# Another pairing of attention heads, and the transfers that follow from it, in a fused attention and feed-forward kernel

## The chip, the cores and the metric

The kernel runs on one core of a Trainium2 chip. The metric is the device time of one execution in microseconds (us). Three timed runs before the change took 405.54, 406.10 and 406.79 us; the median is 406.1 us. A profiled execution of the same program is shown beside them.

The core has engines that each run a queue of their own and wait for each other by semaphores: TensorE (PE in the profile, with its weight loads as PEld), VectorE (DVE), ScalarE (ACT), GpSimd (POOL) and SyncE (SP). SP computes nothing here; it issues transfers, in the order of its queue. The transfers run on 16 DMA engines.

## The reference

Attention with normalised queries and keys, then a feed-forward layer with a gated activation:

```python
# q, k, v: (8, 12, 448, 64) float32; w_in: (768, 2048); w_out: (2048, 768)
q_n = q / (np.linalg.norm(q, axis=-1, keepdims=True) + 1e-06)
k_n = k / (np.linalg.norm(k, axis=-1, keepdims=True) + 1e-06)
scores = np.matmul(q_n, k_n.transpose(0, 1, 3, 2)) / tau          # tau = 0.1
scores = scores - np.max(scores, axis=-1, keepdims=True)
attn = np.exp(scores)
attn = attn / (np.sum(attn, axis=-1, keepdims=True) + 1e-09)
attn_out = np.matmul(attn, v)
x = attn_out.transpose(0, 2, 1, 3).reshape(B * S, H * D)          # (3584, 768)
h = x @ w_in
g = h * np.clip(h + 3.0, 0.0, 6.0) / 6.0
out = g @ w_out                                                   # (3584, 768) float32
```

## The kernel before

**Pairs and twins.** The 12 heads of a batch are worked on in 6 pairs, so there are 48 pairs in all, numbered i = 0 to 47. A pair is worked on as one: its two heads fill the 128 rows of a tile, 64 each, in the transposed queries and keys and in the transposed attention output `xT`, whose chunk `hp` of 128 rows is the left operand's contraction in the first feed-forward product. Which two heads make a pair therefore decides which rows of `w_in` belong to which partition. In the kernel before, pair n of a batch holds heads n and n + 6. Two pairs, 2d and 2d + 1, make a twin d.

**Items.** The inputs of a twin's attention are loaded as two items j = 2d and 2d + 1, one of q and one of k; there are 48 items of 448 KB (four heads of 448 x 64 float32). An item's tile has 128 partitions: 64 for each of the two pairs of the twin, and on each partition, for both heads g = 0, 1 of the pair, seven rows of 64 numbers (1,792 bytes in one piece of memory). `load_qk` (line 189) issues an item's load on SP. The seven buffers `raws` (five from item 26 on) hold items; a load waits until the item that used its buffer last has been normalised (line 190).

An item is then squared (`square`, line 211, on ACT, POOL or DVE), reduced to sums of squares on DVE (`reduce`, line 228), its inverse norms are made on ACT (`norms`, line 246), and it is multiplied by them (`normalise`, line 266, mostly on POOL). It is transposed by TensorE at first and, from item 14 on, by a crossbar transfer that SP issues (`crossbar`, line 325). `scores`, `exps` and `values` (lines 395, 428, 453) make the attention of a pair, and `back_crossbar` or `back_two` (lines 504, 515) bring its output into `xT`, again by crossbar transfers on SP.

**Values.** `load_v` (line 201) loads a twin's four heads by four transfers on SP: for each g the two heads of that place in their pairs, and for each of them the two halves of the sequence, on 64 partitions each, shifted against each other so that both end in tiles of 4 x 64 numbers. Zeros are put beside them at the start (lines 966 to 968). `vcast` (line 285) turns a pair's two heads into bf16 on POOL or DVE; before, they lie at places i % 2 and i % 2 + 2 of the twin's tile.

**Weights.** `next_weights` (line 908) issues the next entry of a list on POOL's queue, which also casts float32 to bf16: four pieces of `w_in`, then four of `w_out`, each of 768 KB in bf16. A piece of `w_in` before is one half of the partitions (g) for one half of the columns (f). The assertion in `mm1_unit` (line 563) says how many pieces must have been issued before a unit may run: two for the first eight units of a batch, four for the others.

**Order.** Everything up to pair 17 follows a plan written out by hand (`PLAN`, line 21): LQ is `load_qk`, LV `load_v`, SQ, RE, NO, NM the steps of an item, XD the crossbar transpose, W the next weights, U a unit of the feed-forward layer. From pair 18 on a loop (line 999) goes over the pairs; units of the feed-forward layer (`mm1_unit`, `product_unit`, `single_unit`) are put between the steps of attention so that TensorE always has work. In iteration i the item i + 5 is squared on POOL (line 1034), item i + 3 normalised and pair i + 2's values cast on POOL (line 1046), items i + 2 and i + 3 transposed in even iterations (lines 1028 and 1048), item i + 5 reduced on DVE and item i + 7 loaded (line 1050); in odd iterations the values of a later twin are loaded (line 1052). SP's queue holds all of these transfers and the stores of results (`result`, line 595, line 602) in the order of the program. Behind the loop come the units that are left (line 1061).

Of the kernel before, what the change touches and what calls it, by code (L numbers as in the profile page):

```python
# [61 lines left out]
def kernel(  # L62
# [10 lines left out]
    nc = tc.nc  # L73
    B, H, S, D = q.shape
    d_model, d_ff = moe_w_in.shape
    inv_tau = 1.0 / float(tau)

    HP = H // 2
    NP = B * HP
    CC = d_model // 128  # L80
    FCN = d_ff // 128
# [3 lines left out]
    assert (S, D, HP, SR) == (448, 64, CC, 64)  # L85


    w_in_r = moe_w_in.tensor.rearrange("(g n p) f -> g p n f", g=2, p=64)
    w_out_r = moe_w_out.tensor.rearrange("(fc p) m -> p fc m", p=128)

    const = ctx.enter_context(tc.tile_pool(name="const", bufs=1))
# [7 lines left out]
    w_in_sb = const.tile([128, CC, d_ff], BF16, name="w_in_sb", tag="w_in_sb")  # L99
# [10 lines left out]
    XJ = 14  # L110
# [7 lines left out]
    NV, NR = 3, 7  # L118
# [5 lines left out]
    def item(n):  # L124
        return big[:, n * RAW : (n + 1) * RAW].rearrange("p (g c d) -> p g c d", g=2, c=7)

    vr = [
        big[:, c : c + VAL].rearrange("p (i c d) -> p i c d", i=4, c=5)
        for c in range((NR + 2) * RAW, (NR + 2) * RAW + NV * VAL, VAL)
    ]  # L130
# [4 lines left out]
    def raw_before(j):  # L135

        return j - NR if j < 26 else j - NR + 2

    def raw_buffer(j):
        return raws[j % NR if j < 26 else (j - 26) % (NR - 2)]  # L140
# [22 lines left out]
    raw_of, sq_of, nrm_of, at_of, on_of = {}, {}, {}, {}, {}  # L163
# [3 lines left out]
    def needs(*what):  # L167
        for w in what:
            assert w in issued or any(x < 0 for x in w[1:] if isinstance(x, int)), w
# [3 lines left out]
    def whole(op, j, heads):  # L173

        done = halves.setdefault((op, j), set())
        done.update(heads)
        if len(done) == 2:
            issued.add((op, j))
        return len(done) == 2
# [9 lines left out]
    def load_qk(j, *heads):  # L189
        needs(("NM", raw_before(j)))  # L190
        raw_of[j] = raw_buffer(j)
        d = j // 2
        b, n = 2 * d // HP, 2 * d % HP
        f = (q, k)[j % 2 ^ (j >= XJ)][b].rearrange("(g n) (p c) d -> n p g (c d)", g=2, c=7)[n : n + 2]
        f = f.rearrange("n p g x -> (n p) g x")
        g = slice(heads[0], heads[0] + 1) if heads else slice(0, 2)
        nc.sync.dma_start(out=raw_of[j][:, g, :, :].rearrange("p g c d -> p g (c d)"), in_=f[:, g, :])
        whole("LQ", j, heads or (0, 1))
        issued.update(("LQ", j, x) for x in heads or (0, 1))

    def load_v(d):
        needs(("VC", 2 * (d - NV)), ("VC", 2 * (d - NV) + 1))
        b, n = 2 * d // HP, 2 * d % HP
        for g in range(2):
            f = v[b, HP * g + n : HP * g + n + 2].rearrange("i (p c) d -> p i (c d)", c=7)
            t = vr[d % NV][:, 2 * g : 2 * g + 2, :, :].rearrange("p i c d -> p i (c d)")
            for half in range(2):
                o = t[64 * half : 64 * half + 64, :, (1 - half) * D : (5 - half) * D]
                nc.sync.dma_start(out=o, in_=f[:, :, 3 * half * D : (3 * half + 4) * D])

    def square(j, e, c0, n):

# [71 lines left out]

    def vcast(i, e):
        needs(("LV", i // 2), ("VA", i - NVX, 3))
        t = vr[i // 2 % NV][:, i % 2, 1:5, :]
        f = bass.AP(tensor=t.tensor, offset=t.offset, ap=[t.ap[0], [9 * D, 2], [D, 4], [1, D]])
        o = vx[i % NVX][:, :, 0:D].rearrange("p (g c) d -> p g c d", g=2)
        if e == "v":  # L290
            nc.vector.tensor_reduce(out=o, in_=f.rearrange("p g c (d x) -> p g c d x", x=1), axis=AX.X, op=ALU.max)
            return
        (engines[e].copy if e == "a" else engines[e].tensor_copy)(out=o, in_=f)  # L293
# [4 lines left out]
    def bank_of(name, reads):  # L298

        bank = {"Y": Y, "Z": Z}[name] if name else next_bank()  # L300
        key = id(bank)
        assert not unread.get(key), name
        unread[key] = reads
        return bank, key
# [235 lines left out]
    def g_of(b):  # L540
        if b == B - 1:
            needs(("NM", NP - 1), ("RE", NP - 1), ("VC", NP - 1))
            return g_last
        return gT[b % 2]
# [15 lines left out]

    def mm1_unit(b, fc):
        needs(*(("CX", i) for i in range(b * HP, (b + 1) * HP)))
        assert len(weights) <= 6 - 2 * (2 * fc // FCN)
        x, g, c0 = xT[b % 2], g_of(b), b % 2 * SR
        ps, key = bank_of(None, 1)
        for cc in range(CC):
            nc.tensor.matmul(  # L567
                ps[:, 0:S],
                w_in_sb[:, cc, fc * 128 : (fc + 1) * 128],
                x[:, cc, 0:S],  # L570
                start=(cc == 0),
                stop=(cc == CC - 1),
            )
        def relu():
            u = sb.tile([128, S], BF16, name="u", tag="u", bufs=3)
            nc.scalar.activation(  # L576
                out=u[:, :], in_=ps[:, 0:S], func=AF.Relu, bias=half_bias, scale=1.0 / 6.0
            )
            post["v"].append(lambda: product(u))

        def product(u):
            nc.vector.scalar_tensor_tensor(  # L582
                out=g[:, fc, c0 : c0 + S],
                in0=u[:, :],
                scalar=1.0,
                in1=ps[:, 0:S],
                op0=ALU.min,
                op1=ALU.mult,
            )
            unread[key] = 0  # L590
            g_done.add((b, fc))

        post["a"].append(relu)
# [41 lines left out]
    def firsts(b, *fcs):  # L635
        return [(mm1_unit, b, fc) for fc in fcs]
# [236 lines left out]
    for b in range(2, B - 1):  # L873
        first = firsts(b, *range(FCN))
        for n, x in enumerate([0, 3, 3, 3, 3, 2]):
            i = (b + 1) * HP + n
# [3 lines left out]
            if i == NP - 1:  # L880
                p, last = [last], None
            x = 0 if n == 1 else 1 if n in (0, 5) and i > FIRST else 2
# [5 lines left out]
    b = B - 1  # L888
    f = firsts(b, *range(FCN))
# [3 lines left out]
    for n, x in enumerate("2176"):  # L893
# [4 lines left out]
    units[NP] += [(product_unit, n, x, 2) for n, x in ((9, "7"), (9, "6"), (10, "6"))]  # L898
    units[NP] += [(product_unit, 10, "7", x) for x in range(2)]

    FG = d_ff // 2
    weights = [
        (w_in_sb[64 * g : 64 * g + 64, :, f * FG : (f + 1) * FG], w_in_r[g, :, :, f * FG : (f + 1) * FG])
        for f in range(2)
        for g in range(2)
    ] + [(w_out_sb[:, 4 * f : 4 * f + 4, :], w_out_r[:, 4 * f : 4 * f + 4, :]) for f in range(4)]

    def next_weights():
# [31 lines left out]
    def whole_units(n, engines="av"):  # L940
# [5 lines left out]

    OPS = {
        "LQ": load_qk, "LV": load_v, "W": next_weights, "SQ": square, "RE": reduce, "NO": norms,
        "NM": normalise, "VC": vcast, "TR": transposes, "XD": crossbar, "XB": back_crossbar, "XP": back_two, "CQ": copy_q, "CK": copy_k, "CS": copy_k3, "SC": scores,
        "EX": exps, "VA": values, "FI": finish_values, "BK": back, "CX": copy_x, "U": unit, "UA": lambda: finish_units("a"), "UV": lambda: finish_units("v"),  # L950
        "GL": g_left, "WS": lambda x, *h: weight_sums(str(x), *((h[0] * KC // 2, KC // 2) if h else (0, KC))), "UU": whole_units, "D": busy, "DP": busy_pv, "OPEN": open_ring,
# [12 lines left out]


    for t in vr:
        nc.vector.memset(t[64:128, 0:2, 4, :], 0.0)
        nc.vector.memset(t[0:64, 2:4, 0, :], 0.0)
    zeros = xT[1][:, 0, :]
    nc.vector.memset(zeros, 0.0)  # L970
    nc.vector.memset(eps_bias, EPS)
# [27 lines left out]
    for i in range(FIRST, NP):  # L999
# [36 lines left out]
        n = 2  # L1036
# [61 lines left out]
```

## Time and profile before

| | |
|---|---|
| median of three runs | 406.1 us |
| the profiled execution | 404.91 us, of which the span is 403.1 |
| TensorE's granted clock in it | 1.00 |
| read from and written to memory | 47.19 MB and 11.01 MB |
| q and k loads | 24 and 24 of 448 KB, 4.4 and 4.9 us from issue to landing (median) |
| value loads | 96 of 128 KB, 4.4 us |
| input weights | 4 of 768 KB, 10.2 us |
| stores of results | 114 in all, of 96 KB (110) and 48 KB (4), 2.0 to 2.4 us |
| crossbar transposes | 34 of items, 3.3 us; 25 of attention outputs, 3.8 us |

The profile comes from one execution. The span runs from the first to the last instruction. A share such as "PE 98%" is that engine's busy time over the span. The DMA line cuts the span into 40 slices of some 10 us, and each digit is the mean busy share of the 16 DMA engines in tenths. The chain goes back from the last instruction, at each step to what released it. Rows of transfers give the time from issue to landing; the time of an issue itself is what SP or POOL spends on it.

### The profile page before, as it was taken

The page shows a single profiled execution, that of the slowest core. Times are in us where ns is not written, and L with a number is a line of the kernel's source. Part 1 is how long each engine was busy: PE and PEld are TensorE (multiplying, and loading weights), DVE is VectorE, ACT ScalarE, POOL GpSimd, SP SyncE. Part 2 cuts the span into 40 slices and gives each one's busy share as a digit, 9 for nine tenths or more (in the row PEclk, how much of TensorE's full clock was granted, in tenths as well). Part 3 has the DMA queues.
Part 4 walks back from the last instruction along what each step waited for, and adds up shares of the span by engine and source line. Part 5 has one row for each costly group of instructions (what it writes and reads, how often), then busy time and mean ns, then how long its engine had stood idle before and what let it go on. Part 6 is the DMA issues. An engine that isn't in the chain of part 4 may idle for free.

```text
span 403.1 us, 9619 instructions
## 1 busy us (share of the span) xinstructions
PE 395.5 (98%) x3696; PEld 234.3 (58%) x3696; DVE 286.4 (71%) x503; ACT 278.3 (69%) x609; POOL 234.0 (58%) x228
## 2 busy tenths in 40 slices
PE   7999999999999999999999999999999999999996
PEld 4666656555655556556555556555565556555563
DVE  5898768766998777776867888687656566644663
ACT  5999998798467686786858768668658755225230
POOL 7799655662384997488386865766665500510070
PEclk9999999999999999999999999999999999999999
DMA  8999989979988659786989659976963523130134
GB/s 289 281 254 257 216 247 230 156 125 230 187 213 220 139 128 228 171 222 130 180 216 212 152 130 164 182 192 145 192 154 76 112 46 67 41 79 21 26 73 99
DMA packets 91566, 65.32 MB, mean 162 GB/s; under 512 B 56064, under 2 KB 89984, under 8 KB 91520
## 3 DMA queue, kind: packets, MB, share of 16 engines
q1 hardware_dynamic: 87408, 58.02, 62.8%
q0 software_dynamic: 3712, 6.29, 9.0%
q8 instruction: 29, 0.48, 0.5%
q10 hardware_dynamic: 400, 0.39, 0.3%
q14 instruction: 17, 0.14, 0.1%
HBM read 47.19 MB, written 11.01 MB: 144 GB/s over the span
## 4 chain that ended last, share of the span: by engine, by line
PE 94%; DVE 3%; DMA 1%; ACT 0%; issue 0%; DVEq 0%; ACTq 0%
PE M L567 24%; PE M L740 17%; PE PV L462 13%; PE Y L567 6%; PE M L422 6%; PE Z L567 5%; PE Y L740 4%; PE Z L740 4%; PE M L614 3%; PE M L820 2%; PE Z L422 2%; PE PV L922 2%; PE Z L820 1%; PE Y L422 1%; DVE n L238 1%; PE SC L422 1%
## 5 line engine op out<-in xcount | busy, mean ns | idle before, releaser
L440 ACT ACTIVATE at<-M 128x448 bf16<-128x448 f32 x200 | 99.9, 568 | 16.4 <-PE M L422 14.4
L567 PE MATMUL M<-xT,w_in_sb 128*128 128x448 bf16 x522 | 110.8, 352 | 0.0
L567 PEld LDWEIGHTS <-w_in_sb 128*128 128x128 bf16 x768 | 72.0, 98 | 62.6 <-issue 2.8
L274 POOL TENSOR_TENSOR nrm<-big,r 128x896 bf16<-128x896 f32 (+1 forms) x48 | 79.5, 1662 | 26.1 <-ACT r L262 19.3
L576 ACT ACTIVATE u<-M,bias 128x448 bf16<-128x448 f32 x87 | 57.0, 655 | 25.2 <-PE M L567 24.8
L582 DVE SCALAR_TENSOR_TENSOR gT<-u,M 128x448 bf16<-128x448 bf16 x76 | 46.7, 618 | 36.8 <-ACT u L576 36.3
L226 POOL TENSOR_TENSOR big<-big 128x896 f32<-128x896 f32 (+3 forms) x39 | 63.9, 1641 | 10.9 <-DMA big<-in_k_dram 5.7
L462 PEld LDWEIGHTS <-at 128*128 128x128 bf16 (+1 forms) x1536 | 54.9, 97 | 22.8 <-issue 13.5
L462 PE MATMUL PV<-vx,at 128*128 128x65 bf16 (+1 forms) x1536 | 64.3, 194 | 0.2 <-DVE on L483 0.2
L238 DVE TENSOR_REDUCE n<-big 128x14 f32<-128x896 f32 (+1 forms) x50 | 51.7, 1041 | 5.6 <-ACT big L224 4.6
L379 POOL COPY km<-tT 64x128 bf16<-64x128 bf16 x34 | 12.8, 376 | 58.1 <-DMA tT<-nrm 45.1
L769 POOL TENSOR_TENSOR big<-big 128x384 f32<-128x384 f32 x11 | 11.8, 1076 | 54.6 <-ACT big L788 54.5
L740 PEld LDWEIGHTS <-gT 128*128 128x128 bf16 x288 | 27.8, 98 | 20.0 <-DVE gT L718 0.6
L740 PE MATMUL M<-w_out_sb,gT 128*128 128x384 bf16 x208 | 37.9, 326 | 0.1
L440 ACT ACTIVATE at<-Z 128x448 bf16<-128x448 f32 x49 | 27.7, 565 | 9.9 <-PE M L422 7.3
L483 DVE TENSOR_TENSOR on<-PV,rc 128x512 bf16<-128x512 f32 x48 | 33.2, 691 | 1.7
L293 POOL CAST vx<-big 128x512 bf16<-128x512 f32 x44 | 33.2, 757 | 1.2 <-DMA big<-in_v_dram 1.1
L422 PE MATMUL M<-tT,kz 64*128 64x448 bf16 (+1 forms) x175 | 31.6, 351 | 0.0
L740 PEld LDWEIGHTS <-gs 128*128 128x128 bf16 x224 | 21.5, 98 | 14.8 <-DVE gs L718 0.4
L567 PE MATMUL Y<-xT,w_in_sb 128*128 128x448 bf16 x132 | 28.6, 352 | 0.0
L440 ACT ACTIVATE at<-Y 128x448 bf16<-128x448 f32 x45 | 25.7, 570 | 3.1 <-PE Z L422 1.7
L740 PE MATMUL M<-w_sum,gs 128*128 128x384 bf16 x144 | 26.3, 326 | 0.0
(130 smaller groups left out, 561.7 us busy)
## 6 DMA issues: line engine op xcount, KB each, us to landing
big<-in_v_dram SPq DMA_DIRECT2D x96, 128.0 KB, 4.4
big<-in_k_dram SPq DMA_DIRECT2D x24, 448.0 KB, 4.9
big<-in_q_dram SPq DMA_DIRECT2D x24, 448.0 KB, 4.4
out_dram<-o SPq DMA_DIRECT2D x107, 96.0 KB, 2.2
w_in_sb<-in_moe_w_in_dram POOLq DMA_DIRECT2D x4, 768.0 KB, 10.2
w_out_sb<-in_moe_w_out_dram POOLq DMA_DIRECT2D x4, 768.0 KB, 9.2
tT<-nrm SPq DMA_TRANSPOSE x34, 3.3
xT<-on SPq DMA_TRANSPOSE x25, 3.8
```

What stands on the lines that cost most here:

```text
L226: engines[e].tensor_tensor(out=o, in0=i, in1=i, op=ALU.mult)
L238: nc.vector.tensor_reduce(out=n2s[d % 2][:, j % 2, c], in_=sq[:, :, :, :].rearrange("p g c d -> p (g c) d")[:, c, :], axis=AX.X, op=ALU.add,)
L274: engines[e].tensor_tensor(out=nrm[:, :, g, :].rearrange("p c g d -> p g c d"), in0=raw_of[j][:, g, :, :], in1=rs[d % 2][3][:, j % 2, :] . ...
L293: (engines[e].copy if e == "a" else engines[e].tensor_copy)(out=o, in_=f)
L422: nc.tensor.matmul(o, ks, qt[rows], start=True, stop=True)
L440: nc.scalar.activation(out=o, in_=x, func=AF.Exp, scale=inv_tau)
L462: nc.tensor.matmul(pv_out(j, h), at[rows, n, q_cols(i // HP, j)], vt[rows, 3 + h if name == "M" else 5 * h + int(name[1]), :], start=(name ...
L483: nc.vector.tensor_tensor(out=on[:, :, :, :].rearrange("p j h d -> p h j d"), in0=pv4[:, :, :, 0:D], in1=rc[:, :, :].to_broadcast([128, 2, ...
L567: nc.tensor.matmul(ps[:, 0:S], w_in_sb[:, cc, fc * 128 : (fc + 1) * 128], x[:, cc, 0:S], start=(cc == 0), stop=(cc == CC - 1),)
L576: nc.scalar.activation(out=u[:, :], in_=ps[:, 0:S], func=AF.Relu, bias=half_bias, scale=1.0 / 6.0)
L582: nc.vector.scalar_tensor_tensor(out=g[:, fc, c0 : c0 + S], in0=u[:, :], scalar=1.0, in1=ps[:, 0:S], op0=ALU.min, op1=ALU.mult,)
L740: nc.tensor.matmul(m, lhs[:, c, :], rhs[:, c, c0 : c0 + width], start=(base is None and c == 0), stop=(c == KC - 1), skip_group_check=True,)
```

## The change

Pair n of a batch now holds the neighbouring heads 2n and 2n + 1. Rows 128 n to 128 n + 127 of `w_in` then belong to chunk n as they stand, so a piece of `w_in` is a quarter of the columns on all 128 partitions. A twin's four heads lie side by side, so its values are loaded by two transfers, one for each half of the sequence, with four heads in each; a pair's two heads lie at places 2(i % 2) and 2(i % 2) + 1 of the tile. An item of q or k is loaded by two transfers, one for each place g in the pair, each of which takes the two heads 2n + g and 2n + 2 + g.

```diff
-    w_in_r = moe_w_in.tensor.rearrange("(g n p) f -> g p n f", g=2, p=64)
+    w_in_r = moe_w_in.tensor.rearrange("(n p) f -> p n f", p=128)
...
-        f = (q, k)[j % 2 ^ (j >= XJ)][b].rearrange("(g n) (p c) d -> n p g (c d)", g=2, c=7)[n : n + 2]
-        f = f.rearrange("n p g x -> (n p) g x")
-        g = slice(heads[0], heads[0] + 1) if heads else slice(0, 2)
-        nc.sync.dma_start(out=raw_of[j][:, g, :, :].rearrange("p g c d -> p g (c d)"), in_=f[:, g, :])
+        f = (q, k)[j % 2 ^ (j >= XJ)][b].rearrange("(n g) (p c) d -> g n p (c d)", g=2, c=7)
+        for g in heads or (0, 1):
+            o = raw_of[j][:, g, :, :].rearrange("p c d -> p (c d)")
+            nc.sync.dma_start(out=o, in_=f[g, n : n + 2])
...
-        for g in range(2):
-            f = v[b, HP * g + n : HP * g + n + 2].rearrange("i (p c) d -> p i (c d)", c=7)
-            t = vr[d % NV][:, 2 * g : 2 * g + 2, :, :].rearrange("p i c d -> p i (c d)")
-            for half in range(2):
-                o = t[64 * half : 64 * half + 64, :, (1 - half) * D : (5 - half) * D]
-                nc.sync.dma_start(out=o, in_=f[:, :, 3 * half * D : (3 * half + 4) * D])
+        f = v[b, 2 * n : 2 * n + 4].rearrange("i (p c) d -> p i (c d)", c=7)
+        t = vr[d % NV][:, :, :, :].rearrange("p i c d -> p i (c d)")
+        for half in range(2):
+            o = t[64 * half : 64 * half + 64, :, (1 - half) * D : (5 - half) * D]
+            nc.sync.dma_start(out=o, in_=f[:, :, 3 * half * D : (3 * half + 4) * D])
...
-        t = vr[i // 2 % NV][:, i % 2, 1:5, :]
-        f = bass.AP(tensor=t.tensor, offset=t.offset, ap=[t.ap[0], [9 * D, 2], [D, 4], [1, D]])
+        t = vr[i // 2 % NV][:, 2 * (i % 2), 1:5, :]
+        f = bass.AP(tensor=t.tensor, offset=t.offset, ap=[t.ap[0], [4 * D, 2], [D, 4], [1, D]])
...
-        assert len(weights) <= 6 - 2 * (2 * fc // FCN)
+        assert len(weights) <= 7 - 4 * fc // FCN
...
-    FG = d_ff // 2
+    FG = d_ff // 4
     weights = [
-        (w_in_sb[64 * g : 64 * g + 64, :, f * FG : (f + 1) * FG], w_in_r[g, :, :, f * FG : (f + 1) * FG])
-        for f in range(2)
-        for g in range(2)
+        (w_in_sb[:, :, f * FG : (f + 1) * FG], w_in_r[:, :, f * FG : (f + 1) * FG]) for f in range(4)
     ] + [(w_out_sb[:, 4 * f : 4 * f + 4, :], w_out_r[:, 4 * f : 4 * f + 4, :]) for f in range(4)]
...
     for t in vr:
-        nc.vector.memset(t[64:128, 0:2, 4, :], 0.0)
-        nc.vector.memset(t[0:64, 2:4, 0, :], 0.0)
+        nc.vector.memset(t[64:128, 0:4:2, 4, :], 0.0)
+        nc.vector.memset(t[0:64, 1:4:2, 0, :], 0.0)
```

## The prediction

> **What bounds the kernel now.** I read the page first (busy shares, the line of DMA shares, the chain), then stretches of the trace, the order of time of SP's queue and of POOL, and at last the record of the DMA packets by size.
>
> ```profile
> span 403.1 us, 9619 instructions
> PE 395.5 (98%) x3696; PEld 234.3 (58%) x3696; DVE 286.4 (71%) x503; ACT 278.3 (69%) x609; POOL 234.0 (58%) x228
> ...
> DMA  8999989979988659786989659976963523130134
> ...
> q1 hardware_dynamic: 87408, 58.02, 62.8%
> q0 software_dynamic: 3712, 6.29, 9.0%
> ...
> PE 94%; DVE 3%; DMA 1%; ACT 0%; issue 0%; DVEq 0%; ACTq 0%
> ```
>
> TensorE works 395.5 of 403.1 us and holds 94% of the chain: only 7.6 us can be won without taking work from it. The DMA line is at 8 to 9 tenths through the first third and 72% over the span, so the transfers stand close behind. They must keep pace, but no wait for them decides today (1% of the chain).
>
> Two stretches of the span (length, busy time and count of PE, PEld, DVE, ACT, POOL, granted clock, DMA share, GB/s):
>
> ```profile
> 4.00:6.00 2.00, 2.00 (x12) 1.44 (x11) 1.58 (x4) 1.16 (x3) 1.18 (x2) 1.00 1.04 398
> ...
> 296.00:403.00 107.00, 103.19 (x774) 60.34 (x772) 60.29 (x99) 48.49 (x98) 27.87 (x28) 1.00 0.31 69
> ```
>
> In 4 to 6 us almost nothing but q and k loads moves: 398 GB/s with all 16 engines occupied (share 1.04), 24.9 GB/s for each. From 296 us on the engines are at 0.31.
>
> Of SP's issues by line (ns at least, median, at most) and of the order of time of SP and of POOL:
>
> ```profile
> L197 SPq DMA_DIRECT2D big<-in_k_dram x24: 367/584/1504, 0.7 to 281.1; - x24
> L197 SPq DMA_DIRECT2D big<-in_q_dram x24: 368/578/1603, 1.3 to 291.0; - x24
> ...
> L209 SPq DMA_DIRECT2D big<-in_v_dram x96: 595/606/1611, 3.8 to 298.7; - x96
> ```
>
> ```profile
> 290.97 0.59 SPq L197 DMA_DIRECT2D big<-in_q_dram  x1
> ```
>
> ```profile
> 295.44 1.68 POOL L226 TENSOR_TENSOR big<-big 128x896 f32<-128x896 f32 x1
> ```
>
> The last of the 48 loads is issued at 290.97 us and squared at 295.44; behind that square 403.1 - 295.4 = 107.7 us of the program follow.
>
> **The change, part by part.** The values: 96 transfers of 128 KB become 48 of 256 KB with the same rows of 1 KB, and the outermost count of their patterns stays 64 on both sides. SP issues 48 fewer at 0.606 us: -29 us of SP. The q and k loads: 48 transfers become 96 at 0.58 us: +28 us of SP. Together nothing, in the same places of the queue. The input weights: four transfers of 768 KB stay four, on 128 partitions with rows of half the length; in the trace they are issued on POOL from 23.07 to 42.89 us at 0.70 us each and land in 10.2. The first product with them starts at 42.85 us and needs one piece now instead of two; the ninth and thirteenth, at 58.6 and 66.1, need the pieces issued at 40.0 and 42.9, which land at 50.2 and 53.1. That cover of 8 and 13 us hides them; if rows of half the length doubled the 10.2 us, the third would be 1.8 us late once. I take nothing. The zero fills and the casts of the values keep count and size; nothing.
>
> What is left is the shape of a q or k load. Before, heads n and n+1 lay side by side in memory, so (n p) was one dimension: source and target patterns were 128 x 2 x 448. Now each transfer takes heads g+2n and g+2n+2, whose rows don't join: the built program has 2 x 64 x 448 on the source and 128 x 1 x 448 on the target. Rows stay 1,792 B and the bytes the same. The question is over how many of the 16 engines such a transfer is shared. The trace has no transfer of that kind: every load and store in it has an outermost count of 64 or 128 on both sides. So the cost is bounded from both sides. If the split goes by single rows, 16 engines take part and a load costs what it does now. If it goes by the outermost count, both sides can be cut alike only into 2 (2 and 128 share no larger divisor than 2), and two engines carry every q and k load.
>
> I take the second. Issuing costs SP 0.58 us for 256 rows, 0.61 for 128 (values) and 0.56 for 64 (a store, line 602): the time doesn't grow with the rows, so what deals the work out doesn't walk over rows but steps through a pattern, and its outermost step is the only one that is large in all transfers seen to fill 16 engines.
>
> The Trainium skill, "DMA: Bandwidth & Descriptors", section "Why a DMA increments its semaphore by 16 and not by 1", says this outright: the number of engines is the largest up to 16 that divides the outermost counts of both patterns, and on this kind of queue they are the lowest-numbered ones. By that rule each half load runs on the same two engines and the sum below holds; without it the time is that of the first rival. No run here shows it yet.
>
> **The sum.** Two engines are then the bound. Their work until the last load has landed, from the packet record, median of one packet (mean in brackets); where a transfer uses all 16 engines, one carries a sixteenth:
> - q and k: 12,288 packets of 1,792 B, half on each, 6,144 x 74 ns = 455 us (95 ns: 585). As a check, at 24.9 GB/s for each engine 22.0 MB take 442.
> - crossbar transposes: 54 of 59 lie ahead; 49,920 packets of 256 B, 3,120 x 54/59 x 18 ns = 51 us (25 ns: 72).
> - values: 736 packets of 1 KB at 46 ns = 34 us (63: 46).
> - stores: 62 of 114 lie ahead of the last load, 4 packets each, 248 x 119 ns = 30 us (110: 27).
> - weights: 128 packets at 135 ns and 96 at 173 = 34 us (36); semaphore writes 5 us.
>
> That is 609 us (771 by the means). I take the medians: the means hold the crowding of 16 busy engines at 162 GB/s, and 65.3 MB in some 720 us are 91 GB/s. With 0.7 us to the first issue, some 2 to the first packet and the 107.7 behind the last load: 719 us of span, 1.8 us around it as now (404.9 against 403.1). The profiled execution is 1.2 us under the median of 406.1, which doesn't matter here: **720 us**.
>
> Do the two engines ever run dry? A load is needed by the square of iteration i (line 1034, POOL, item i+5). Behind that square on POOL stand the normalising of i+3 and a value cast; the normalising releases the transpose on SP (line 1048) and then load i+7 (line 1050): 1.68 + 1.69 + about 1.3 us, some 5 us after load i+5 landed. Load i+6 was issued an iteration earlier and keeps the engines for 9.5 us. On DVE the reduce of i+5 (line 1050) holds up the next iteration's evacuations, and these TensorE by the banks; TensorE needs 395.5/48 = 8.2 us an iteration, the engines 609/48 = 12.7. So the queue stays filled with some 4 us to spare; TensorE's waiting is the other side of it. Before the loop up to seven buffers are filled ahead.
>
> **Rivals.**
> 1. All 16 engines, as today. For it: bytes, row length and rows are unchanged, and nothing in the trace shows a narrower transfer. Against it: the issue times above. TensorE then stays the bound; the decisive point is whether a half load still passes in about 0.6 us (229 KB at 398 GB/s). SP's -29 and +28 us cancel; at best the 7.6 us without TensorE work shrink, less the 2.48 us ahead of its first matmul: 400 to 407 us, 405 likeliest. This is the case that is not slower.
> 2. Two engines, and the queue runs dry in the loop. From load 24 on, a load would be issued only once its iteration's TensorE work is done, so the two follow each other: 24 x 8.2 = 197 us more, 916 us. For it: only two loads are under way in the loop, and TensorE may run slower behind long waits (its first 18 matmuls of 248 columns took 3.90 us, 217 ns each; thirteen later ones 1.54 us, 118 each). Against it: the 4 us to spare.
>
> Between forecast and the second rival lie partial mixtures and the means of the packets: 771 + 110 = 881.
>
> **How the numbers follow.** Forecast 0.80, rival one 0.12, rival two 0.08. The range holds the forecast's unknown costs: below, if packets of two queues overlap as shares of up to 1.15 in the trace allow, 609/1.15 + 110 = 640; above, 881 by the means, and some of rival two's mixtures. It leaves out rival one and most of rival two, 0.2 together: 640 to 880. Less than 0.3% (1.2 us) can't be told from no change by a measurement of this kernel. Rival one splits as 0.05 faster, 0.05 within 0.3%, 0.02 slower; everything else is slower: 0.90.
>
> **What would show it.** Right: q and k loads take 9 us and more from issue to landing (4.4 to 4.9 now); the mean DMA share falls to about a third while bytes stay at 65.3 MB; TensorE's busy time stays near 395 us, about 55% of the span, and its idle time hangs by POOL squares and DVE reduces that wait for `big<-in_q_dram` and `big<-in_k_dram`; transposes and values land late as well, since their sixteenth on the two engines stands in the same line; the last load lands near 610 us. Wrong: loads landing in 3 to 5 us and a DMA line like today's. If the shares are low but the span is over 880, rival two or slow packets did it: the landing times of a pair of halves (9.5 us, or more) tell which.

## The result, and the profile after

The changed kernel takes 729.13 us (median of four runs, 728.85 to 730.28), against 405.82 for the kernel before in the same runs: 1.797 times as long, with a 95% interval of 1.793 to 1.800. The forecast was 720 us, in a range of 640 to 880.

From the page of the changed kernel (the engines' busy time, the 40 slices for the granted clock and the transfers, bytes by queue, the chain):

```profile
span 728.5 us, 9613 instructions
PE 453.8 (62%) x3696; PEld 255.9 (35%) x3696; DVE 278.5 (38%) x503; ACT 282.8 (39%) x609; POOL 229.2 (31%) x228
...
PEclk8556555768957797859867889768876987999999
DMA  1122144642537957867398397778778739832313
...
q1 hardware_dynamic: 86064, 58.02, 51.6%
...
DMA 36%; SPq 29%; PE 24%; POOL 4%; DVE 3%; issue 3%; ACT 1%; POOLq 0%; DVEq 0%; ACTq 0%
```

The same bytes are moved (58.02 MB on this queue before and after). TensorE has fallen from 98% of the span to 62%, and from 94% of the chain to 24%. In its place the chain holds transfers (36%) and SP (29%).

Two stretches, with the columns explained at the prediction:

```profile
20.00:50.00 30.00, 5.79 (x32) 3.43 (x33) 5.33 (x9) 3.97 (x9) 4.50 (x5) 0.50 0.13 51
...
625.00:728.00 103.00, 99.12 (x750) 57.91 (x748) 58.51 (x96) 45.55 (x91) 28.51 (x28) 1.00 0.33 73
```

From 20 to 50 us, where nearly nothing but q and k loads is under way, the mean share of the 16 engines is 0.13 and the rate 51 GB/s. Two engines of 16 are 0.125, and two at the 24.9 GB/s that one had before are 49.8. The last 103 us look like the last 107 of the kernel before: TensorE at work for 96% of them, the transfers at a third.

SP's issues by line, then the order of time on SP at the start and on POOL at the last square of an item:

```profile
L197 SPq DMA_DIRECT2D big<-in_k_dram x48: 533/3183/8953, 0.7 to 594.3; - x48
L197 SPq DMA_DIRECT2D big<-in_q_dram x48: 515/592/10970, 2.1 to 616.2; - x48
```

```profile
0.74 1.30 SPq L197 DMA_DIRECT2D big<-in_k_dram  x2
2.09 7.26 SPq L197 DMA_DIRECT2D big<-in_q_dram  x2
9.39 8.87 SPq L197 DMA_DIRECT2D big<-in_k_dram  x2
18.30 8.87 SPq L197 DMA_DIRECT2D big<-in_q_dram  x2
```

```profile
627.49 1.68 POOL L225 TENSOR_TENSOR big<-big 128x896 f32<-128x896 f32 x1 [7.08 <-DMA big<-in_q_dram]
```

The first item's halves go out at once (1.30 us); from the second item on SP is held in the issue itself, in this stretch 8.87 us for the two halves of an item. That is the time in which two engines move them: 458,752 bytes in 8.87 us are 51.7 GB/s. Over the whole run it comes and goes: the median issue is 3,183 ns for k and 592 ns for q. The last item is squared at 627.49 us instead of 295.44, after a wait of 7.08 us that its load ended, and 101.0 us follow instead of 107.7.

Who waited for whom, longest in total first (us in all, times, longest):

```profile
POOL big L225 <- DMA big<-in_q_dram: 166.4, 17, 31.9
DVE n L237 <- POOL big L225: 135.2, 27, 29.2
POOL km L378 <- DMA tT<-nrm: 132.3, 15, 12.6
```

The waits begin at the loads (POOL's squares), go on to the reduces on DVE, and the crossbar transposes are late as well: the copies behind them wait 132.3 us in all, against 45.1 before.

### The profile page after: what moved, and what is told of

It reads as the page before. It is cut to its first block, busy times and chain, and to the rows that moved or that the text cites. A ratio compares the mean times of both kernels' runs of the same rounds, so it can differ in the third digit from the quotient of the medians.

```text
span 728.5 us, 9613 instructions
## 1 busy us (share of the span) xinstructions
PE 453.8 (62%) x3696; PEld 255.9 (35%) x3696; DVE 278.5 (38%) x503; ACT 282.8 (39%) x609; POOL 229.2 (31%) x228
## 3 DMA queue, kind: packets, MB, share of 16 engines
q1 hardware_dynamic: 86064, 58.02, 51.6%
## 4 chain that ended last, share of the span: by engine, by line
DMA 36%; SPq 29%; PE 24%; POOL 4%; DVE 3%; issue 3%; ACT 1%; POOLq 0%; DVEq 0%; ACTq 0%
DMA big<-in_q_dram 20%; SPq L197 18%; PE M L566 8%; SPq L329 6%; PE M L739 6%; DMA xT<-on 5%; DMA big<-in_k_dram 4%; DMA tT<-nrm 4%; DMA big<-in_v_dram 3%; PE PV L461 2%; SPq L208 2%; PE Y L739 2%; PE Z L566 2%; POOL big L225 2%; SPq L519 2%
## 5 line engine op out<-in xcount | busy, mean ns | idle before, releaser
L566 PE MATMUL M<-xT,w_in_sb 128*128 128x448 bf16 x522 | 125.7, 384 | 72.0 <-DMA xT<-on 56.6
L566 PEld LDWEIGHTS <-w_in_sb 128*128 128x128 bf16 x768 | 77.6, 105 | 149.2 <-issue 99.0
L461 PE MATMUL PV<-vx,at 128*128 128x65 bf16 (+1 forms) x1536 | 72.3, 204 | 29.3 <-POOL vx L292 27.3
L461 PEld LDWEIGHTS <-at 128*128 128x128 bf16 (+1 forms) x1536 | 62.1, 104 | 60.3 <-issue 49.2
L421 PE MATMUL M<-tT,kz 64*128 64x448 bf16 (+1 forms) x175 | 37.2, 401 | 32.4 <-DMA tT<-nrm 31.6
L378 POOL COPY km<-tT 64x128 bf16<-64x128 bf16 x34 | 12.4, 363 | 138.9 <-DMA tT<-nrm 132.3
L421 PEld LDWEIGHTS <-kz 64*128 64x128 bf16 (+1 forms) x296 | 15.0, 98 | 115.3 <-DVE kz L368 48.3
L223 ACT ACTIVATE big<-big 128x896 f32<-128x896 f32 (+4 forms) x12 | 9.1, 770 | 95.3 <-DMA big<-in_k_dram 79.0
L368 DVE COPY kz<-tT 128x384 bf16<-128x384 bf16 x34 | 10.5, 347 | 79.9 <-DMA tT<-nrm 79.9
L566 PE MATMUL Y<-xT,w_in_sb 128*128 128x448 bf16 x132 | 32.0, 383 | 0.0
L439 ACT ACTIVATE at<-SC 128x896 bf16<-128x896 f32 (+1 forms) x24 | 19.0, 819 | 31.8 <-PE SC L418 25.8
```

The lines of the kernel that those rows point to most:

```text
L421: nc.tensor.matmul(o, ks, qt[rows], start=True, stop=True)
L439: nc.scalar.activation(out=o, in_=x, func=AF.Exp, scale=inv_tau)
L461: nc.tensor.matmul(pv_out(j, h), at[rows, n, q_cols(i // HP, j)], vt[rows, 3 + h if name == "M" else 5 * h + int(name[1]), :], start=(name ...
L566: nc.tensor.matmul(ps[:, 0:S], w_in_sb[:, cc, fc * 128 : (fc + 1) * 128], x[:, cc, 0:S], start=(cc == 0), stop=(cc == CC - 1),)
```

## The experiments

Theory: a transfer is dealt out along the outermost counts of its two patterns, so that 2 and 128 leave two engines, and these two are the bound. The rivals beside it: the doubled number of transfers, the pairing with its value and weight transfers, or SP's being held. All times are medians; the kernel before stood at 405.4 to 405.8 us in the same runs.

**Only the cut changed: e1.** The changed kernel, with the two transfers of an item cut by pairs.

```diff
-        f = (q, k)[j % 2 ^ (j >= XJ)][b].rearrange("(n g) (p c) d -> g n p (c d)", g=2, c=7)
-        for g in heads or (0, 1):
-            o = raw_of[j][:, g, :, :].rearrange("p c d -> p (c d)")
-            nc.sync.dma_start(out=o, in_=f[g, n : n + 2])
+        f = (q, k)[j % 2 ^ (j >= XJ)][b].rearrange("(n g) (p c) d -> n p g (c d)", g=2, c=7)
+        assert not heads
+        for x in range(2):
+            o = raw_of[j][64 * x : 64 * x + 64, :, :, :].rearrange("p g c d -> p g (c d)")
+            nc.sync.dma_start(out=o, in_=f[n + x])
```

> The changed kernel, with an item still loaded by two transfers of 224 KB and the same rows, but one for each pair (64 partitions, both heads of the pair) instead of one for each place in the pair: the outermost count is 64 on both sides instead of 2 and 128. Theory (two engines carry a transfer whose outermost counts are 2 and 128): all 16 engines again, about 405 us, between 400 and 408, DMA line near 9 tenths at the start, q and k loads landing in 3 to 6 us. Rivals: if the number of transfers, the neighbouring pairs, the value loads or the quarters of the input weights cost the time, it stays near 729 us, or keeps the part of the 323 us that belongs to them.

Measured: 408.41 us, 1.007 (1.004 to 1.010) times the kernel before. From its page:

```profile
span 406.6 us, 9617 instructions
...
DMA  7999999999998848887699759977983522230134
...
big<-in_k_dram SPq DMA_DIRECT2D x48, 224.0 KB, 4.6
big<-in_q_dram SPq DMA_DIRECT2D x48, 224.0 KB, 4.4
```

With as many transfers, of the same size and rows, the engines are full again and a half lands in 4.4 to 4.6 us. So 321 of the 323 us belong to the cut of the q and k loads. The doubled number, the pairing, the value transfers and the quarters of the weights leave 0.7% on balance, and with it e1 ends 0.4 us past the expectation's 408.

**Only the number changed: e2.** The kernel before, an item loaded in two transfers of 128 partitions x 448.

```diff
-        g = slice(heads[0], heads[0] + 1) if heads else slice(0, 2)
-        nc.sync.dma_start(out=raw_of[j][:, g, :, :].rearrange("p g c d -> p g (c d)"), in_=f[:, g, :])
+        for g in heads or (0, 1):
+            o = raw_of[j][:, g, :, :].rearrange("p c d -> p (c d)")
+            nc.sync.dma_start(out=o, in_=f[:, g, :])
```

> The kernel before, with an item loaded by two transfers of 224 KB, one for each place in the pair; since heads n and n + 1 lie side by side, the pattern is 128 x 448 on both sides. Theory: 16 engines, 405 to 408 us. Rival (twice as many transfers of half the size on SP cost the time): near 729 us, at least well above 420.

Measured: 407.76 us, 1.005 (1.003 to 1.007). Twice as many transfers cost 2 us, not 323.

**The outermost count alone: e3 to e6.** The kernel of e2, with the same number of transfers, sizes and rows; only the source is written as k groups of 128/k rows. So that they can't be joined, each group starts a row early. For k = 4:

```diff
+            r = f[:, g, :]
+            r = bass.AP(tensor=r.tensor, offset=r.offset, ap=[[31 * 7 * D, 4], [7 * D, 32], [1, 7 * D]])
-            nc.sync.dma_start(out=o, in_=f[:, g, :])
+            nc.sync.dma_start(out=o, in_=r)
```

> The kernel before, with an item loaded by two transfers of 224 KB whose source is written as 2 x 64 rows of 448 numbers; the second group starts one row early, so that the two can't be joined into one count of 128 (one row is read twice and the last one left out: the output isn't the reference's). Pairing, values and weights are those of before. Theory: two engines, as in the changed kernel, 715 to 745 us, 48 to 52 GB/s and a DMA share of 0.125 where q and k alone move. Rival (the pairing, or the distance of two heads in memory, costs the time): 405 to 410 us.

> As the one with 2 x 64, but 4 x 32 rows (three rows read twice; the output isn't the reference's). Theory: four engines; one of them carries 3072 packets of 1,792 B at 80 ns, 246 us, and 154 of the rest, 400 us until the last load, and 101 to 108 behind it: 495 to 520 us; 96 to 104 GB/s and a DMA share of 0.25 at the start. Rival (any split pattern costs the same, whatever its count): 729 us.

> As the one with 2 x 64 and the one with 4 x 32, with 8 x 16 rows (seven rows read twice; the output isn't the reference's). Theory: eight engines; one of them carries 1536 packets at 80 ns, 123 us, and 154 of the rest, 277 us until the last load, less than the 294 us at which the last load lands in the kernel before. TensorE is the bound again, with waits in the first 100 us where the loads are densest: 407 to 430 us. Rival (any outermost count under 16 holds the loads back, as the whole transfer stands behind the slowest engine): above 440 us.

> The same with 16 x 8 rows (fifteen rows read twice; the output isn't the reference's). Theory: 16 engines, the time of two transfers of 128 x 448, 406.5 to 409.5 us. Rival (the form of the pattern, three counts instead of two, costs something of its own, on SP or in the engines): above 411 us.

| | outermost count of the source | us | last square at | from there to the end |
|---|---|---|---|---|
| e3 | 2 | 717.40 (one run) | 614.8 | 100.8 |
| e4 | 4 | 513.20 (one run) | 410.1 | 101.3 |
| e5 | 8 | 442.31, ratio 1.092 (1.084 to 1.099) | 332.8 | 106.2 |
| e6 | 16 | 410.37, ratio 1.014 (1.009 to 1.019) | 299.7 | 107.4 |
| e2 | 128 | 407.76, ratio 1.005 (1.003 to 1.007) | 299.3 | 107.1 |

The stretch from 4 to 6 us of e3, e4, e5 and e6, each from its own run:

```profile
4.00:6.00 2.00, 2.00 (x12) 1.44 (x11) 0.00 (x0) 0.00 (x0) 0.00 (x0) 1.00 0.13 51
```

```profile
4.00:6.00 2.00, 2.00 (x12) 1.44 (x11) 0.00 (x0) 0.00 (x0) 0.08 (x1) 1.00 0.26 98
```

```profile
4.00:6.00 2.00, 2.00 (x12) 1.44 (x11) 0.00 (x0) 0.00 (x0) 0.51 (x1) 1.00 0.49 147
```

```profile
4.00:6.00 2.00, 2.00 (x12) 1.44 (x11) 1.14 (x3) 1.15 (x3) 0.27 (x1) 1.00 0.93 242
```

The share of engines doubles with the count: 0.13, 0.26, 0.49, 0.93, that is 2, 4, 8 and 15 to 16 of 16. The packets of 4 bytes (the semaphore writes in the prediction's list) give the same count exactly. On SP's queue e2 has 6,704 of them and e3 to e6 have 5,360, 5,552, 5,936 and 6,704; these are 14, 12, 8 and 0 fewer for each of the 96 loads, as if each engine that takes part writes one. The changed kernel has 14 fewer for each than e1. e3 brings nearly the whole loss (717 us) into the kernel before by the writing of one pattern, so pairing and memory distance are out. e3 and e4 fell into their ranges. e5 didn't: 442 us against 407 to 430, and inside its rival's range (above 440). The expectation took 80 ns a packet; in e5 the packets of q and k took 100.7 ns in the mean and those of the transposes 29.7 (medians 74 and 18). With such means one engine's work until the last load is, as an estimate, 1,536 x 100.7 + 2,640 x 29.7 ns + 105 to 125 us of the rest, some 340 to 360 us, enough for a last square at 332.8. The rival (a transfer waits for its slowest engine) gives the same sign; how much belongs to which isn't settled. e6, at 410.4 us, lies between its two ranges (up to 409.5, and above 411), so a small cost of the three-count form is neither shown nor excluded.

**From POOL's queue: e7.** The line that issues reads `nc.gpsimd.dma_start` in the changed kernel.

> The changed kernel, with the q and k loads issued on POOL's queue instead of SP's, the patterns unchanged (2 x 64 on the source). Theory A (a narrow transfer takes the same two engines whoever issues it): 710 us and more. Theory B (on this queue each transfer takes the next two engines in turn, as the Trainium skill says in the page DMA: Bandwidth & Descriptors, section on the increment by 16): four to eight engines work on the halves that are under way, 410 to 480 us with POOL busy for some 75 us more (96 issues at 0.7 to 0.8 us).

Measured: 566.1 us (one run), in neither range. From 12 to 14 us the two halves of the first item move, beside the last few packets of SP's value loads:

```profile
12.00:14.00 2.00, 0.00 (x0) 0.00 (x0) 0.00 (x0) 0.00 (x0) 0.00 (x0) 0.79 0.25 100
...
big<-in_k_dram POOLq DMA_DIRECT2D x48, 224.0 KB, 10.6
big<-in_q_dram POOLq DMA_DIRECT2D x48, 224.0 KB, 11.0
```

A share of 0.25 and 100 GB/s are four engines. The two halves alone have 34 packets of 5,376 bytes in these 2 us, at some 215 ns each 7.3 us of work, so they have these four between them and not the same two. Theory A falls on this queue, and the engine count is that of B. B's time is missed by 86 us. One thing that it left out is POOL's own order:

```profile
3.49 1.74 POOL L197 DMA_DIRECT2D big<-in_k_dram  x2
14.90 0.51 POOL L225 TENSOR_TENSOR big<-big 128x192 f32<-128x192 f32 x1 [9.67 <-DMA big<-in_k_dram]
15.35 1.61 POOL L197 DMA_DIRECT2D big<-in_q_dram  x2
```

The second item's load is issued at 15.35 us, behind a square that waits for the first. The packets differ too: a transfer is moved in 42 packets of 5,376 bytes and 2 of 1,792, with 294 of 12 bytes beside them, not in 128 rows of 1,792. How much of the 566 us either of these makes, and why a half takes 10.6 to 11.0 us to land, stays open.

**From two queues: e8.** Half of the loads issued by ACT.

```diff
-            nc.sync.dma_start(out=o, in_=f[g, n : n + 2])
+            (nc.scalar if g else nc.sync).dma_start(out=o, in_=f[g, n : n + 2])
```

> The changed kernel, with the half of each item for place g = 1 issued on ACT's queue, patterns unchanged. In the changed kernel SP was held in the issue of q and k loads for much of the span, and stores and transposes stand behind them. Theory A (the work of two engines is the bound and SP's being held only follows from it): 700 to 760 us. Theory B (SP's being held is the bound, so that two queues share it): under 600 us.

Measured: 709.17 us (one run). The stretch from 10 to 20 us:

```profile
10.00:20.00 10.00, 0.25 (x3) 0.00 (x0) 1.57 (x3) 0.67 (x2) 0.51 (x1) 0.69 0.13 51
```

Both queues have loads under way in it (202 and 81 packets), and together they get 0.13 and 51 GB/s: they feed the same two engines. SP's being held, 29% of the chain, follows from those; sharing it saves 20 us.

**The last 0.7%: e9 and e10.** In e1, the second half of the first items issued by ACT (e9: six items, where the plan has them; e10: four, ahead of ACT's first square).

```diff
-            nc.sync.dma_start(out=o, in_=f[n + x])
+            (nc.scalar if x and j < 6 else nc.sync).dma_start(out=o, in_=f[n + x])
```

> The kernel of e1_cut_by_pair (neighbouring pairs, 16 engines), with the second half of the first six items issued on ACT's queue, so that the first loads are issued as early as in the kernel before. e1 took 0.7% more than the kernel before, and its TensorE worked 7.2 us of the stretch from 10 to 20 us where the kernel before has 9.35. Theory (the extra issues at the start delay the first items by 2 to 3 us): 405 to 406.5 us, with 9 us or more of TensorE in that stretch. Rival (the extra comes from the loads' later places in SP's queue all along, or from wider crowding of the engines): 407.5 to 409 us as in e1.

> As e9, but for the first four items alone and with their issues ahead of the first square on ACT's queue (in e9 they stood between the squares). Theory (the extra issues at the start delay the first items): 405 to 407 us, with 9 us or more of TensorE from 10 to 20 us. Rival (the extra comes from later in the program): 407.5 to 409 us, as in e1.

Measured: e9 413.91 us, 1.020 (1.019 to 1.022); e10 409.06 us, 1.009 (1.007 to 1.010). In e9 the order on ACT shows the mishap: the second item's half is issued at 5.38 us, behind a square that waits for the first.

```profile
0.77 0.76 ACTq L198 DMA_DIRECT2D big<-in_k_dram  x1
5.33 0.36 ACT L224 ACTIVATE big<-big 128x192 f32<-128x192 f32 x1 [3.30 <-DMA big<-in_k_dram]
5.38 0.63 ACTq L198 DMA_DIRECT2D big<-in_q_dram  x1
```

e10 has no such order, and still gains nothing. The stretch from 10 to 20 us of the kernel before, e2, e1 and e10, each from its own run:

```profile
10.00:20.00 10.00, 9.35 (x108) 6.26 (x106) 8.72 (x15) 9.39 (x18) 7.59 (x6) 1.00 1.05 282
```

```profile
10.00:20.00 10.00, 8.39 (x94) 5.61 (x92) 8.87 (x14) 9.39 (x18) 7.59 (x6) 1.00 1.06 286
```

```profile
10.00:20.00 10.00, 7.20 (x70) 4.60 (x68) 7.22 (x11) 8.29 (x19) 6.77 (x6) 1.00 1.10 238
```

```profile
10.00:20.00 10.00, 7.50 (x73) 4.67 (x72) 7.67 (x12) 9.07 (x20) 7.43 (x7) 1.00 1.10 235
```

TensorE works 7.50 us there in e10, against 7.20 in e1 and 9.35 before, so issuing the first four items earlier doesn't bring the start back. e9 lies outside both of its ranges, and e10 at the top of its rival's (the extra comes from later in the program), which no run tested further. What the start of e1 and e10 shows instead is a lower rate (last section). But that need not be most of the 0.7%: e2, which has none of e1's halves of 64 partitions, is already 2.1 us slower than the kernel before, and e1 2.7. What those 2 us of the doubled transfers consist of stays open. No version here beats the kernel before.

## Why the prediction was right, step by step

- **Two engines.** Shown: the share of 0.13 in the changed kernel, the same loss by one pattern in e3, its end in e1, and the steps of 2, 4, 8 and 16 in between. The argument from issue times was thin support for it: in the changed kernel SP's issue time does grow, to the time of the engines. The Trainium skill has the rule in "DMA: Bandwidth & Descriptors", section "Why a DMA increments its semaphore by 16 and not by 1" (the largest number up to 16 that divides both outermost counts). On SP's queue the shares of 0.13, 0.26, 0.49 and 0.93 agree with it.
- **The work of the two engines.** Forecast 609 us and 2.7 ahead of it, so 612 until the last load; the last square began at 627.5. The term that was too small is q and k: 80.3 ns a packet in the mean instead of the median's 74, 6,144 x 80.3 = 493 us instead of 455. The rest of the list (154 us) had only 627.5 - 493 = 134 us beside it, so part of it overlapped with q and k or was smaller than forecast. One term was: the list has 54 of the 59 transposes ahead of the last load, but the trace before has 50 issued by 292 us, 48 us of work instead of 51.
- **Behind the last load.** Forecast 107.7 us, measured 101.0, and 100.8 to 107.4 in e3 to e6: TensorE is further along when the last load comes late (781 matmuls are left from the last square on in the kernel before, 721 in the changed one). The two misses, +15 and -7 us, leave 729 against 720; that they partly cancel is luck.
- **The engines never run dry.** Rival two (916 us) is out, but the step as written doesn't hold. The packets of q and k, counted in the order of their issue, give the time at which each half had landed. Between 170 and 616 us there are 16 stretches of 0.5 to 7.1 us, 67 us in all, in which every half issued so far had landed and the next wasn't issued yet: the 4 us to spare weren't there in the loop. From 342 to 348 us, for instance, values, stores and transposes are under way instead, work that the sum holds anyway. How much of the 67 us was lost isn't known, since the record doesn't say which engine moved a packet.
- **SP's issues cancel.** That was wrong in two ways. On two engines SP is held, at the start for 8.87 us an item. On 16, e2's doubled loads cost 2 us and e1's, which have the value issues taken off, 2.7, where the forecast had none.
- **What the profile was to show.** TensorE's busy time was to stay near 395 us: it is 453.8, and the granted clock falls to 0.50 in the long waits (the stretch from 20 to 50 us). What that cost isn't separated; TensorE was waiting for most of that time. The mean DMA share was to fall to a third: q1 alone has 51.6%, for a reason that the last section gives. The page has no landing times for these loads; counted from the packets as above, a half landed 6.7 to 26.8 us after its issue, 14.4 in the median, where 9 and more were forecast.
- **The values and the weights at nothing.** Borne out by e1 within its 0.7%.

## What to carry to other kernels

Look at the outermost count of both patterns of a transfer as built, not at its bytes: where two neighbouring dimensions couldn't be joined any more, a count of 2 went to the front, and such a load issued on SP or ACT had 2 of 16 engines here (on POOL's queue the two halves of an item had four). Where a layout needs such a split, cut the transfer so that the partitions' rows stay outermost (e1), and check that the mean share of the engines passes 0.125 where these loads move alone. A narrow transfer delays what stands with it in the queue as well: the transposes here, which use all engines, landed late (132.3 us of waiting behind them instead of 45.1).

## What the runs showed of the hardware that was not expected

- **Packets stand open while two engines are late.** The crossbar transposes are the same 49,920 packets of 256 bytes, 18 ns in the median before and after; but in the mean they take 60.6 ns instead of 25.2, and together 3,027 us instead of 1,259. Only 368 of them are open for over 1 us, and these hold 1,975 us. At 340 us, for instance, 15 are open beside two packets of q and k, so most presumably stand on other engines than those two. The transposes make 0.41 of the DMA share of 0.73 that the changed kernel shows from 200 to 600 us, at 98 GB/s: a high share isn't a high rate.
- **Late loads hold their issuer.** By the same count of packets, an issue of a half took some 0.58 us in the median with at most one half under way, and 4.41 with three.
- **Halves of 64 partitions moved slower than whole 128.** The stretch from 4 to 6 us of e1, where only halves of 64 partitions move:

```profile
4.00:6.00 2.00, 2.00 (x12) 1.44 (x11) 0.73 (x2) 0.67 (x2) 0.74 (x1) 1.00 1.04 246
```

The share is that of the kernel before in the same stretch (1.04), but the rate is 246 GB/s instead of 398, with the same rows of 1,792 bytes. A packet took 115 ns in the median there, against 74 in the kernel before and in e2, whose halves have the same size but 128 partitions. Over the whole run it is 104 ns against 74. A second case is e7 from 4 to 6 us, where only value loads move, onto 64 partitions with rows of 1,024 bytes:

```profile
4.00:6.00 2.00, 2.00 (x12) 1.44 (x11) 0.00 (x0) 0.00 (x0) 1.23 (x2) 1.00 1.09 222
```

Their packets take 79 ns in the median, against 46 over the run in the kernel before, where these loads move among others. The number of partitions isn't the only thing that lowers a rate: e6, with 128 partitions, has 242 GB/s from 4 to 6 us, at a median of 74 ns and a mean of 109. The Trainium skill, "DMA: Bandwidth & Descriptors", section "Rules for kernel authors", advises one transfer of 128 partitions rather than two of halves, as they use the same engines. The advice fits this case, and the rule gives no figure for the loss. The lower rate fits the late start of e1 and e10, though no run removed it alone.
